# K's cache ahead of the MLP's first weights in the load queue of a one-token decode kernel

## The chip, the cores and the metric

The kernel runs on one core of one Trainium2 chip. The metric is the device time of one execution in microseconds (us). The kernel before took 99.68 us, the median of three runs (99.55, 99.68 and 99.71).

## The reference

One token passes through an attention branch and an MLP branch that both start from the same normalised row; their outputs are added to the row itself.

```python
# x: 1x1x1024; wq: 1024x4096; wo: 4096x1024; w1: 1024x3584; w2: 3584x1024, all bf16
# caches: 1 x 4 heads x 65536 x 128; W = 4096, so only the last 4096 positions count
def _A_ref(x, k_cache, v_cache, wq, wo):
    q = (x @ wq) as 32 heads of 128            # 8 query heads share one cache head
    k, v = the last W rows of each cache head
    p = _softmax(q . k * (Dh ** -0.5))
    return (p @ v, heads side by side) @ wo

def _B_ref(x, w1, b1, w2, b2):
    y = _layernorm(x)
    h = _gelu(y @ w1 + b1)
    return h @ w2 + b2

x = A_x
xn = _layernorm(x)
return x + _A_ref(xn, ...) + _B_ref(xn, ...)
```

The MLP branch normalises a second time: its `y` is the layernorm of `xn`.

## The kernel before

**Work and data.** With one token there is no reuse: each weight and each cache row is read once, 39.86 MB in all. TensorE multiplies the row by the weights in tiles 32 columns wide, four side by side. The order of every engine's instructions is the order in which the program writes them, and all waits are semaphores that are written out by hand.

**The load queue.** All large transfers are issued by SyncE (SP), in this order: W1 (7.34 MB, `w1_p`, line 208), K in two transfers of 2.10 MB (`load_cache(KR, ...)`, line 199), Wq in two of 4.19 MB (`load_rows(WA, wq_p, ...)`, line 191). SP then waits until h is done (line 366) and issues W2 into W1's place (line 367) and V in two transfers of 2.10 MB. It waits until q is done and issues Wo into Wq's place in four transfers of 5.24, 2.10, 0.79 and 0.26 MB. The three small rows, b1 (7 KB), x (2 KB) and b2 (2 KB), are issued by ScalarE, in this order, on a queue of its own (lines 204 to 206).

**The row.** x arrives (semaphore `s_xrow`); TensorE turns it into a column (line 289); VectorE, GpSimd and ScalarE do both layernorms on it (lines 292 to 316), which gives `XNTb` for q and `YTb` for h. VectorE then clears half of PSUM (line 318).

**h.** TensorE adds b1 (line 353) and waits for `YTb` and for W1; a rolled loop does 8 steps of 7 products (`h_rows`, line 358). ScalarE copies the result (373, 374), TensorE turns it (392), VectorE copies it to `HT` (397) and goes through GELU in small steps (401 to 413) with one exponential on ScalarE (406).

**K.** K's two transfers land in `KR`. VectorE turns them in 8 pieces of 128x2048 (`turn_k`, line 326) from `KR` into `KD`, which lies 2048 columns ahead of `KR` in the same buffer, so that each piece is written over the piece before it, which has been read by then. A piece that starts a transfer (n = 0 and n = 4) waits for that transfer; the others wait for the piece before. In VectorE's order pieces 0 to 2 stand behind line 318, piece 3 between the two halves of GELU, and pieces 4 to 7 behind GELU.

**q and the rest.** TensorE waits for `HT` (line 419), lays a mask into PSUM (422) and does q in two parts of four steps, each when its half of Wq has landed: SP passes on the landing (`s_row`, lines 370, 371). Then follow the turn of q (427 to 450), the scores on `KD` (477), the softmax (480 to 513), h by W2 (515), p by V (528), and the product with Wo (564 to 572), whose rows are taken as Wo's four transfers land. ScalarE copies the sum (579) and writes it out (581).

Of the kernel before, what the change touches and what calls it, by code (L numbers as in the profile page):

```python
# [10 lines left out]
D = 1024  # L11
# [39 lines left out]
def bass_parallel_sum__sliding_block_cached__mixer_channel_mlp__decode_kernel(  # L51
# [18 lines left out]
    pe, dve, act, pool, sp = nc.tensor, nc.vector, nc.scalar, nc.gpsimd, nc.sync  # L70

    def sems(name, n):
        return [nc.alloc_semaphore(f"{name}{i}") for i in range(n)]

    s_xrow, s_b1, s_b2, s_w1, s_w2, s_out, s_go, s_row = (
        nc.alloc_semaphore(n) for n in ("s_xrow", "s_b1", "s_b2", "s_w1", "s_w2", "s_out", "s_go", "s_row"))
    s_wq = sems("s_wq", len(WQ_CHUNKS))
    s_k = sems("s_k", NPAIR)
# [4 lines left out]
    DVE = Track(nc, "S_DVE")  # L83
# [3 lines left out]
    def sb(name, shape, d):  # L87
        return nc.alloc_sbuf_tensor(name, shape, d)
# [14 lines left out]
    XBR = sb("XBR", [1, 2 * D], bf16)  # L103
# [27 lines left out]
    KR = KV[:, 2048:2048 + HKV * W]  # L131
# [11 lines left out]
    x_row = A_x.rearrange("b s n -> (b s) n")  # L143
# [44 lines left out]
    def load_rows(dst, src, chunks, width, semaphores):  # L188
        c0 = 0
        for j, n in enumerate(chunks):  # L190
            sp.dma_start(  # L191
                dst[:, c0 * width:(c0 + n) * width].rearrange("p (c n) -> p c n", c=n),
                src[:, c0:c0 + n, :],
            ).then_inc(semaphores[j], 16)
            c0 += n

    def load_cache(dst, cache, semaphores):
        for i in range(NPAIR):
            sp.dma_start(  # L199
                dst[:, 2 * i * W:2 * (i + 1) * W],  # L200
                cache[0, 2 * i:2 * i + 2, SK - W:SK, :].rearrange("g (m b) d -> m g (b d)", m=64),
            ).then_inc(semaphores[i], 16)

    act.dma_start(B1R, b1_row.rearrange("o (c n) -> o c n", c=B1N)).then_inc(s_b1, 16)
    act.dma_start(XBR[:, 0:D], x_row).then_inc(s_xrow, 16)
    act.dma_start(XBR[:, D:2 * D], b2_row).then_inc(s_b2, 16)

    sp.dma_start(W1[:, :], w1_p).then_inc(s_w1, 16)  # L208
    load_cache(KR, A_k_cache, s_k)
    load_rows(WA, wq_p, WQ_CHUNKS, NQ, s_wq)  # L210


# [108 lines left out]
    def turn_k(n):  # L321
        if n % 4 == 0:
            dve.wait_ge(s_k[n // 4], 16)
        else:
            dve.wait_ge(DVE.sem, DVE.cnt)
        C["kd"] = DVE.mark(dve.transpose(  # L326
            out=KD4[:, n], in_=KR[:, n * 2048:(n + 1) * 2048].rearrange("p (b e s) -> p b e s", b=16, e=4)))

# [43 lines left out]
    act.wait_ge(PE.sem, C["h"])  # L372
    C["a_hrow"] = ACT.mark(act.activation(out=Hs[:, 0:512], in_=PS[:, 0:512], func=ACTF.Copy))
    C["a_hrow"] = ACT.mark(act.activation(out=Hs[0:96, 512:1024], in_=PS[0:96, 512:1024], func=ACTF.Copy))
    for n in range(3):
        turn_k(n)

    def q_rows(n):
# [11 lines left out]
    for i in range(8):  # L390
        n = 128 if i < 4 else 96
# [9 lines left out]
    DVE.mark(dve.scalar_tensor_tensor(out=U2[:, :], in0=HT[:, :], scalar=0.044715, in1=HT[:, :], op0=ALU.mult, op1=ALU.mult))  # L401
    dve.wait_ge(DVE.sem, DVE.cnt)
    C["d_T"] = DVE.mark(dve.scalar_tensor_tensor(out=U2[:, :], in0=U2[:, :], scalar=1.0, in1=HT[:, :], op0=ALU.add, op1=ALU.mult))
    turn_k(3)
    act.wait_ge(DVE.sem, C["d_T"])
    C["a_sig"] = ACT.mark(act.activation(out=U2[:, :], in_=U2[:, :], func=ACTF.Exp, scale=-GELU_C))
    dve.wait_ge(ACT.sem, C["a_sig"])
# [4 lines left out]
    dve.wait_ge(POOL.sem, C["consts"])  # L412
    C["d_GT"] = DVE.mark(dve.tensor_tensor(out=GT, in0=HT[:, :], in1=U2[:, :], op=ALU.mult))

    for n in range(4, 8):
        turn_k(n)

    pe.wait_ge(DVE.sem, C["zq"])
    pe.wait_ge(DVE.sem, C["d_HT"])
# [193 lines left out]
```

## Time and profile before

| what | value |
|---|---|
| median of three runs | 99.68 us |
| the profiled execution, its own time | 99.53 us |
| its span in the trace | 98.3 us |
| busy: PE, VectorE, ScalarE, GpSimd | 50%, 32%, 10%, 10% of the span |
| time of the DMA packets on the SP queue | 95.1% of 16 engines' span |
| moved | 39.86 MB, mean 406 GB/s |
| first DMA issue on SP | 0.80 us |
| last product's end, write-out issued | 96.15 us, 96.58 us |

The span runs from the first to the last instruction that the profiler saw, in microseconds from its start; the execution's own time is 1.2 us longer. A DMA is seen twice: as the instruction that issues it (SPq for SP, ACTq for ScalarE), with the time which that takes on the issuing engine, and as its packets on the 16 DMA engines. PE is TensorE's products, DVE is VectorE, ACT is ScalarE, POOL is GpSimd.

### The profile page before, as it was taken

Reading aid. Unit: us, or ns where it says so; the run is one execution under the profiler, and the core shown is the slowest. Engines: PE = TensorE matmul, PEld = TensorE weight load, DVE = VectorE, ACT = ScalarE, POOL = GpSimd, SP = SyncE. Lnnn points to the kernel's source line nnn. Section 1 sums busy time; section 2 is a strip of 40 time slices with the busy share of each in tenths; the row PEclk is TensorE's granted clock in tenths of the full one; section 3 lists DMA queues with packets and bytes.
Section 4 is the critical chain, followed back from the end, with each engine's and each line's share of the span. In section 5 each row is a group of like instructions: output and inputs, shape, how many; then the busy total and the mean of one; then the engine's idle time right before and its main releaser. Section 6 shows DMA issues by size and latency. Waiting matters only on the chain.

```text
span 98.3 us, 1233 instructions
## 1 busy us (share of the span) xinstructions
PE 49.0 (50%) x500; PEld 18.4 (19%) x415; DVE 31.5 (32%) x42; ACT 9.6 (10%) x23; POOL 10.1 (10%) x34
## 2 busy tenths in 40 slices
PE   0000022659520700670077589993675599786671
PEld 0000022213110000100010321221433243524240
DVE  0000003270799999993002300415550001300000
ACT  0500000240400000000002200001920001000001
POOL 2000001499940000000000000000000000000000
PEclk9999999999997555559755555999999958999999
DMA  9898888999999999999988889949999979799960
GB/s 350 350 423 373 374 373 374 447 433 427 433 513 440 427 440 440 427 427 427 587 373 373 373 373 513 607 173 427 427 433 513 467 333 533 317 417 427 387 267 1
DMA packets 1773, 39.86 MB, mean 406 GB/s; under 512 B 231, under 2 KB 235, under 8 KB 493
## 3 DMA queue, kind: packets, MB, share of 16 engines
q1 hardware_dynamic: 1728, 39.85, 95.1%
q10 hardware_dynamic: 44, 0.01, 0.1%
q14 instruction: 1, 0.00, 0.0%
HBM read 39.86 MB, written 0.00 MB: 406 GB/s over the span
## 4 chain that ended last, share of the span: by engine, by line
DMA 89%; PE 4%; SPq 4%; issue 1%; ACT 0%
DMA WW<-in_A_wq_dram 47%; DMA WW<-in_A_wo_dram 42%; PE PS L334 4%; SPq L191 2%; SPq L199 1%; ACT ORow L579 0%; SPq L208 0%; SPq L370 0%
## 5 line engine op out<-in xcount | busy, mean ns | idle before, releaser
L326 DVE STREAM_TRANSPOSE KV<-KV 128x2048 bf16<-128x2048 bf16 x8 | 18.5, 2310 | 3.4 <-DMA KV<-in_A_k_cache_dram 3.2
L334 PE MATMUL PS<-WW,XNTb 128*32 x64 | 7.2, 629 | 11.9 <-SPq L370 11.9
L334 PE MATMUL PS<-WW,VEC 128*32 (+1 forms) x240 | 9.5, 275 | 4.9 <-issue 3.2
L334 PE MATMUL PS<-KV,LB 128*128 128x512 bf16 x31 | 9.0, 463 | 1.1 <-DVE LB L450 1.1
L289 PE MATMUL PS<-oneb,XBR 1*128 1x1 bf16 x8 | 0.6, 196 | 13.9 <-DMA XBR<-in_A_x_dram 13.9
L334 PEld LDWEIGHTS PS<-WW,VEC 128*32 (+1 forms) x236 | 5.1, 96 | 9.3 <-issue 9.0
L334 PE MATMUL PS<-KV 128*64 x32 | 5.3, 507 | 1.9 <-DMA KV<-in_A_v_cache_dram 1.9
L334 PE MATMUL PS<-WW,YTb 128*32 x56 | 5.1, 494 | 1.5 <-DMA WW<-in_B_w_dram 1.5
L480 DVE TENSOR_REDUCE MXP<-PS 128x1 f32<-128x1024 f32 x2 | 2.4, 1224 | 8.3 <-PE PS L334 8.3
L292 DVE COPY XT<-PS 128x8 f32<-128x8 f32 x1 | 0.2, 168 | 14.6 <-PE PS L289 14.6
L334 PEld LDWEIGHTS PS<-WW,XNTb 128*32 x32 | 1.2, 114 | 18.4 <-issue 18.4
L541 DVE SCALAR_TENSOR_TENSOR OD<-PS,BLK,OD 128x128 f32<-128x128 f32 x3 | 1.1, 351 | 10.6 <-ACT OD L538 10.5
L334 PE MATMUL PS<-OUTM,PAR 2*128 2x512 bf16 x4 | 1.9, 614 | 4.7 <-DVE HT L397 4.7
L534 PE MATMUL PS<-E,identf 128*128 128x512 f32 x8 | 3.9, 616 | 0.0
L427 DVE CAST Qs<-PS 128x512 bf16<-128x512 f32 x1 | 0.7, 691 | 8.4 <-PE PS L334 8.4
L334 PEld LDWEIGHTS PS<-KV,LB 128*128 128x128 bf16 x16 | 1.9, 117 | 7.7 <-issue 6.9
L510 DVE STREAM_TRANSPOSE KV<-KV 128x512 bf16<-128x512 bf16 x4 | 2.7, 712 | 1.8 <-ACT KV L506 1.8
L334 PEld LDWEIGHTS PS<-KV 128*64 x32 | 2.4, 142 | 4.5 <-issue 4.0
L289 PEld LDWEIGHTS PS<-oneb,XBR 1*128 1x128 bf16 x8 | 0.6, 165 | 13.9 <-issue 13.9
L506 ACT ACTIVATE KV<-PS,BIAS 128x512 bf16<-128x512 f32 x4 | 2.7, 685 | 0.0
L425 ACT ACTIVATE Qs<-PS 128x512 bf16<-128x512 f32 x1 | 0.6, 597 | 20.4 <-PE PS L334 20.4
L334 PEld LDWEIGHTS PS<-WW,YTb 128*32 x32 | 1.5, 107 | 5.4 <-issue 5.2
(93 smaller groups left out, 37.6 us busy)
## 6 DMA issues: line engine op xcount, KB each, us to landing
WW<-in_B_w_dram SPq DMA_DIRECT2D x2, 7168.0 KB, 29.9
WW<-in_A_wq_dram SPq DMA_DIRECT2D x2, 4096.0 KB, 41.7
WW<-in_A_wo_dram SPq DMA_DIRECT2D x1, 5120.0 KB, 35.0
KV<-in_A_k_cache_dram SPq DMA_DIRECT2D x2, 2048.0 KB, 26.0
KV<-in_A_v_cache_dram SPq DMA_DIRECT2D x2, 2048.0 KB, 47.1
WW<-in_A_wo_dram SPq DMA_DIRECT2D x1, 2048.0 KB, 39.5
WW<-in_A_wo_dram SPq DMA_DIRECT2D x1, 768.0 KB, 40.9
WW<-in_A_wo_dram SPq DMA_DIRECT2D x1, 256.0 KB, 41.1
```

The costliest lines, as they stand in the source:

```text
L191: sp.dma_start(dst[:, c0 * width:(c0 + n) * width].rearrange("p (c n) -> p c n", c=n), src[:, c0:c0 + n, :],).then_inc(semaphores[j], 16)
L199: sp.dma_start(dst[:, 2 * i * W:2 * (i + 1) * W], cache[0, 2 * i:2 * i + 2, SK - W:SK, :].rearrange("g (m b) d -> m g (b d)", m=64),).then ...
L289: last = pe.matmul(xt[:, r:r + 1], lhsT=XBR[0:1, r:D:KC], rhs=oneb[0:1, 0:1])
L326: C["kd"] = DVE.mark(dve.transpose(out=KD4[:, n], in_=KR[:, n * 2048:(n + 1) * 2048].rearrange("p (b e s) -> p b e s", b=16, e=4)))
L334: return pe.add_instruction(mybir.InstMatmult(name=nc.get_next_instruction_name(), engine=pe.engine, ins=[lowered(rhs, False), lowered(lhs ...
L425: C["a_qs"] = ACT.mark(act.activation(out=Qs[:, 0:512], in_=PS[:, 6 * 512:7 * 512], func=ACTF.Copy))
L427: C["d_qs"] = DVE.mark(dve.tensor_copy(Qs[:, 512:1024], PS[:, 7 * 512:8 * 512]))
L480: C["mx", half] = DVE.mark(dve.tensor_reduce(out=MXP[:, half:half + 1], in_=PS[:, half * 1024:(half + 1) * 1024], axis=AX.X, op=ALU.max))
L506: C["exp"] = ACT.mark(act.activation(out=Pb[:, n * 512:(n + 1) * 512], in_=PS[:, n * 512:(n + 1) * 512], func=ACTF.Exp, bias=BIAS[:, :], s ...
L510: C["tr", n] = DVE.mark(dve.transpose(out=PT.rearrange("p (i c h) -> p c i h", i=NPAIR, h=16)[:, 16 * n:16 * n + 16], in_=Pb[:, n * 512:(n ...
L534: pe.matmul(PS[:, 3 * 512:4 * 512], lhsT=identf[:, :], rhs=E4[:, 0:512])
L541: C["d_od"] = DVE.mark(dve.scalar_tensor_tensor(out=OD[:, :], in0=PS[:, 4 * 512 + 128 * c:4 * 512 + 128 * c + 128], scalar=BLK[:, c:c + 1] ...
```

## The change

K's two transfers are issued ahead of W1's on SP; x's load is issued ahead of b1's on ScalarE. On VectorE all 8 pieces of K stand together, ahead of the copy to `HT` and of GELU. Every piece now waits for VectorE's own instruction before it; pieces 0 and 4, which waited for their transfer alone, wait for both. No instruction is added or removed, and no tile, size or operand changes.

```diff
+    act.dma_start(XBR[:, 0:D], x_row).then_inc(s_xrow, 16)
     act.dma_start(B1R, b1_row.rearrange("o (c n) -> o c n", c=B1N)).then_inc(s_b1, 16)
-    act.dma_start(XBR[:, 0:D], x_row).then_inc(s_xrow, 16)
     act.dma_start(XBR[:, D:2 * D], b2_row).then_inc(s_b2, 16)
 
+    load_cache(KR, A_k_cache, s_k)
     sp.dma_start(W1[:, :], w1_p).then_inc(s_w1, 16)
-    load_cache(KR, A_k_cache, s_k)
     load_rows(WA, wq_p, WQ_CHUNKS, NQ, s_wq)
...
     def turn_k(n):
         if n % 4 == 0:
             dve.wait_ge(s_k[n // 4], 16)
-        else:
-            dve.wait_ge(DVE.sem, DVE.cnt)
+        dve.wait_ge(DVE.sem, DVE.cnt)
         C["kd"] = DVE.mark(dve.transpose(
             out=KD4[:, n], in_=KR[:, n * 2048:(n + 1) * 2048].rearrange("p (b e s) -> p b e s", b=16, e=4)))
...
-    for n in range(3):
+    for n in range(8):
         turn_k(n)
...
     C["d_T"] = DVE.mark(dve.scalar_tensor_tensor(out=U2[:, :], ...))
-    turn_k(3)
     act.wait_ge(DVE.sem, C["d_T"])
...
     C["d_GT"] = DVE.mark(dve.tensor_tensor(out=GT, in0=HT[:, :], in1=U2[:, :], op=ALU.mult))
 
-    for n in range(4, 8):
-        turn_k(n)
```

## The prediction

> **What bounds the kernel now.** I read the page's slices and chain first, then the chain in order of time.
>
> ```profile
> DMA  9898888999999999999988889949999979799960
> GB/s 350 350 423 373 374 373 374 447 433 427 433 513 440 427 440 440 427 427 427 587 373 373 373 373 513 607 173 427 427 433 513 467 333 533 317 417 427 387 267 1
> ...
> DMA 89%; PE 4%; SPq 4%; issue 1%; ACT 0%
> ```
>
> ```profile
> 0.80 0.38 SPq L208
> ...
> 1.24 0.62 SPq L199
> ...
> 1.90 0.67 SPq L199
> ...
> 3.24 46.23 DMA WW<-in_A_wq_dram
> ...
> 54.73 41.08 DMA WW<-in_A_wo_dram
> ```
>
> The DMA engines are busy from end to end, and the chain is 89% transfer. Next I asked whether the load queue ever runs dry. Issue start plus time to landing, from the list of DMA issues taken issue by issue, gives the landings: W1 0.80 + 19.4 = 20.2, K 25.1 and 30.0, Wq 39.8 and 49.5, W2 66.4, V 71.3 and 76.2, Wo 88.4, 93.3, 95.2 and 95.8 us. Behind W1 that is 39.85 - 7.34 = 32.51 MB in 75.6 us, 430 GB/s, and each step by itself is at that rate: K 2.10 MB in 4.90 us, Wq 4.19 in 9.71, W2 7.34 in 16.97. The order of issue is the order of landing and nothing waits between. (The 173 GB/s slice is a matter of counting: a packet's bytes are booked where the packet starts.) So the end is set by three things alone: when the stream starts, its bytes, and the 0.35 us from the last landing to the last product with the write-out behind it. Reckoned back from W1's landing by W2's 16.97 us, the stream's effective start is 20.23 - 16.97 = 3.26 us.
>
> How it starts, in slices of 0.2 us, shows the first packets 1.0 us after W1's issue began (0.80) and 0.63 us after it ended (1.18):
>
> ```profile
> 1.60:1.80 0.20, 0.00 (x0) 0.00 (x0) 0.00 (x0) 0.00 (x0) 0.00 (x0) 1.00 0.00 0
> 1.80:2.00 0.20, 0.00 (x0) 0.00 (x0) 0.00 (x0) 0.00 (x0) 0.00 (x0) 1.00 7.31 2294
> ```
>
> Last come the engines' timelines, VectorE's rows and then TensorE's, and one row of the waits:
>
> ```profile
> 25.16 7.00 DVE L326 STREAM_TRANSPOSE KV<-KV 128x2048 bf16<-128x2048 bf16 x3 [3.21 <-DMA KV<-in_A_k_cache_dram]
> ...
> 35.66 9.34 DVE L326 STREAM_TRANSPOSE KV<-KV 128x2048 bf16<-128x2048 bf16 x4
> ```
>
> ```profile
> 20.81 5.12 PE L334 MATMUL PS<-WW,YTb 128*32 x56 [1.52 <-DMA WW<-in_B_w_dram]
> ...
> 32.41 1.86 PE L334 MATMUL PS<-OUTM,PAR 2*128 2x512 bf16 x4 [4.71 <-DVE HT L397]
> 40.06 3.60 PE L334 MATMUL PS<-WW,XNTb 128*32 x32 [5.79 <-SPq L370]
> 49.76 3.60 PE L334 MATMUL PS<-WW,XNTb 128*32 x32 [6.10 <-SPq L370]
> ```
>
> ```profile
> PE PS L334 <- DMA KV<-in_A_v_cache_dram: 1.9, 1, 1.9
> ```
>
> TensorE waits for a landing in every stage; the tightest waits are 1.9 us ahead of V and 0.9 us ahead of Wo.
>
> **The change part by part.**
>
> *The stream's bytes and order.* The same bytes pass, so K lands at about 8.4 and 13.3, W1 at 30.3 (where K's second half landed before), and Wq, W2, V and Wo where they did, all plus the shift of the start. That 16 KB packets stand first and not 57 KB ones costs nothing in rate: K 428 GB/s, W2 432, in either order.
>
> *The start.* This is the one term that reaches the end. The first issue on SP is now K's, not W1's. K's took 0.62 and 0.67 us, W1's 0.38. If packets start 0.63 us after the issue's end, as W1's did (and the write-out's at the end: issue over at 97.18, first packet at 97.82), the stream starts 0.616 - 0.375 = 0.24 us later. Lower bound: V's issue of the same shape took 0.55, and the first issue of a group of alike ones is the cheapest (Wo 0.33 against 0.43 for the next), so K's could be 0.55 - 0.09 = 0.46, a shift of 0.08. Upper bound: 0.67 as K's second, 0.29, and the 16 engines, whose first packets began over 1.81 to 2.57 us, could be spread by the ratio of issues more, 0.77 x (0.62/0.38 - 1) = 0.5, which sums to 0.8. Below nothing: W1's first packets took 2.4 to 3.1 us and not the 2.12 of later ones, so up to 0.25 us (the engine that began last) could be won if small packets fill the pipe sooner. I take 0.24, the row of K itself. K's second issue and W1's end by about 2.6 us, while K's first transfer feeds the engines until 8.4, so these cost nothing; should that cover be gone, 0.4 us for W1's.
>
> *x ahead of b1.* x was landed at 13.8 us. b1's, x's and b2's packets and their semaphore writes each let one W1 packet of 2.12 us pass (data at 6.7, 11.2 and 15.6 us). Between K's packets such a turn is 0.61 us, and x now stands first: I take 5 us, bounds 3 and 13.9. The chain from x to the cleared PSUM took 21.94 - 13.91 = 8.0 us, so it ends at 13, as K's second half lands. All of this lies beside the load of W1, and nothing at the end waits for it.
>
> *All of K on VectorE ahead of HT.* 8 pieces by 2.335 us = 18.7 us, from 13 to 31.7. Queued behind them are `HT`, GELU and q's copies; behind `HT` waits TensorE with the mask and q. h starts 0.58 us behind W1, at 30.9, and takes 5.1 us, or 56/32 x 3.60 = 6.3 if all at half clock: done at 36.0 to 37.2. ScalarE's copies and the turn took 27.70 - 25.93 = 1.8 us: `HT` at 38 to 39, VectorE long free. Mask (1.86 + 0.33) until 40 to 41.2, q's first part (3.60) until 44 to 45, ahead of Wq's second half at 49.7. GELU takes 3.5 us more, to 42, and is needed at 69.
>
> *SP.* Behind h's wait stand W2, V and `s_row`. W2 is issued at 36 to 37.2 and not 26.0, with Wq queued until 49.7: 12 us of cover. V's issues end by 39, ahead of Wq's first landing at 40.0. The two waits on DVE's own semaphore that pieces 0 and 4 gain cost what the others have between them, 2.335 - 2.310 = 0.03 us.
>
> Sum against the profiled execution: 99.53 + 0.24 = 99.77. It lies 0.15 below the median of the runs shown, so for a median 99.68 + 0.24 = 99.92 us.
>
> **The rivals.**
>
> *A, not slower: the start is counted from the issue's beginning.* Both readings fit the one W1 row (1.0 us from its beginning, 0.63 from its end). If descriptors go out as they are made, K's longer issue is hidden behind its own first packets: shift 0, 99.68. It decides if K's first packet stands before 1.9 us. Against it: the write-out's packet came 1.24 us after its issue began and 0.64 after it ended. The Trainium skill, "DMA: Bandwidth & Descriptors", section "Latency and other measured facts", gives one first-byte latency of about 600 ns for such queues and names no shape; with one latency for every shape, counted from the beginning, the sum is 99.68. The trace's 0.63 us agrees with it, but counted from the end.
>
> *B, faster: the pipe fills sooner.* The 0.25 us above is won and the issue's price is not paid: 99.43. It needs both.
>
> *C, VectorE late.* If x landed at X, the pieces end at X + 8.0 + 18.7, and `HT`, mask and first part of q (0.4 + 1.9 + 3.9) at X + 32.9. That reaches 49.7 only at X = 16.8, and V's wait gives another 1.9 us. At X = 13.9 3 us are left. Had x to wait for W1 again (20 us), the price would be about 1.3 us by TensorE, 101.2; Wo, issued at 53.4 for a place at 76.2, would still not be late.
>
> *D, TensorE at half clock at the end.* Granted clock, third figure from the end:
>
> ```profile
> 44.26:47.68 3.41, 0.00 (x0) 0.00 (x0) 0.73 (x1) 0.00 (x0) 0.00 (x0) 1.00 0.98 422
> 47.68:61.33 13.65, 9.33 (x55) 2.53 (x35) 1.48 (x4) 1.13 (x3) 0.00 (x0) 0.50 0.98 425
> 78.40:81.81 3.41, 3.41 (x20) 1.56 (x18) 0.00 (x0) 0.00 (x0) 0.00 (x0) 0.50 1.22 528
> ```
>
> A stretch of idleness is followed by half clock, and work by full. Before, TensorE idles 6.1 us ahead of q's second part; now 49.9 - 44.5 = 5.4. Should that keep it warm, the scores end earlier, the wait for V grows, and V and Wo could meet a cold TensorE. Wo's 16 products take 0.87 us a step with the gap; q's as many columns took 0.90 at half clock, 1.15 with the gap: 8 steps by 0.28 = 2.2, less 0.6 of slack, about 1.6 us, 101.5. Against it: 5.4 us is still longer than a stretch of 3.41. The Trainium skill, "TensorE: Matmul & The Clock Gate", section "Part 1: The HAM clock gate (the "warmup" mystery)", says that one idle window of about 3.4 us, running free of the kernel, gates the clock; by that rule a gap of 5.4 us holds a whole window in 58% of executions, one of 6.1 in 79%. The rows' 3.41 us agrees.
>
> That the change does not do what it says is excluded for order: K's issues stand ahead of W1's on SP and all 8 pieces ahead of `HT` on VectorE.
>
> **How the numbers follow.** 0.2% is 0.20 us, about what a measurement of this kernel can tell from no change. Forecast 0.62: most of its spread (0.08 to 0.8) is above 0.20, so 0.44 slower, 0.18 the same. A 0.16, the same. B 0.12, faster. C 0.03 and D 0.07, slower. Slower 0.44 + 0.10 = 0.54, same 0.34, faster 0.12. The range goes from 99.55, which takes in A and half of B, to 100.30, which takes in most of the spread and leaves C and D out. The forecast's own range is 99.76 to 100.3.
>
> **What would show it.** In the profile after: K's issue first on SP, 0.6 us long; first packets near 2.05 us; K landed at 8.4 and 13.3, W1 at 30.3, Wo's last part 0.24 us later than 95.81; VectorE through with K by 33 us; TensorE's waits for Wq, V and Wo still there. First packets at 1.8 us say A. An empty stretch in the DMA row or a wait of TensorE for VectorE behind 49 us says that I am wrong about the cover, and a last row that ends later than 0.4 us after Wo's last landing says D.

## The result and the profile after

The changed kernel took 99.95 us (median of 8 runs, 99.86 to 100.3) against 99.60 us for the kernel before (8 runs, 99.44 to 99.71): ratio 1.0042, 95% interval 1.0028 to 1.0056. It is slower by 0.35 us, and the interval does not reach 1. The forecast was 99.92 us, slower. The profiled execution took 100.02 us with a span of 98.8 us, against 99.53 and 98.3.

The page's slices for the kernel after:

```profile
DMA  2799999988899999999998889949999899799960
GB/s 54 292 428 438 451 458 627 441 372 372 372 411 425 425 438 451 478 451 425 567 441 372 372 372 418 627 196 425 425 431 557 382 415 531 315 408 431 382 268 1
```

The row is as full as before, but for the first slice: 54 GB/s where 350 stood. Much of that drop is counting. A packet's bytes are booked where it starts, and K's packets have 16 KB where W1's had 57. The chain in order of time shows where the stream begins and ends:

```profile
0.80 0.63 SPq L199
...
2.11 1.08 SPq L209
...
55.28 41.03 DMA WW<-in_A_wo_dram
```

K's issue takes 0.63 us. The last transfer lands at 55.28 + 41.03 = 96.31 us, against 54.73 + 41.08 = 95.81: 0.50 us later, which is the whole difference of the two profiled executions (100.02 - 99.53 = 0.49). The slices of 0.2 us (the last two figures are the DMA share and GB/s) show that this was there from the first packet on:

```profile
2.00:2.20 0.20, 0.00 (x0) 0.00 (x0) 0.00 (x0) 0.00 (x0) 0.00 (x0) 1.00 0.00 0
2.20:2.40 0.20, 0.10 (x2) 0.13 (x3) 0.00 (x0) 0.00 (x0) 0.00 (x0) 1.00 3.44 655
```

K's first packet starts at 2.21 us, where W1's started at 1.81. VectorE and TensorE, in their timelines, and one row of the waits:

```profile
10.46 18.81 DVE L325 STREAM_TRANSPOSE KV<-KV 128x2048 bf16<-128x2048 bf16 x8
39.49 0.26 DVE L396 CAST HT<-PS 128x16 f32<-128x16 bf16 x2 [10.22 <-PE PS L391]
```

```profile
31.16 6.53 PE L333 MATMUL PS<-WW,YTb 128*32 x56 [22.56 <-DMA WW<-in_B_w_dram]
...
41.06 3.28 PE L333 MATMUL PS<-WW,XNTb 128*32 x32
50.31 3.60 PE L333 MATMUL PS<-WW,XNTb 128*32 x32 [5.97 <-SPq L369]
```

```profile
PE PS L333 <- DMA KV<-in_A_v_cache_dram: 3.8, 1, 3.8
```

VectorE has turned all of K at 29.3 us and then stands idle for 10 us until h's sum has been turned. q's second part waits for Wq as before, and TensorE's wait for V is longer, not shorter (3.8 against 1.9 us). No engine became late for the stream.

### The profile page after: what moved, and what is told of

It is laid out like the page before. It is cut to its first block, busy times and chain, and to the rows that moved or that the text cites. A ratio compares the mean times of both kernels' runs of the same rounds, so it can differ in the third digit from the quotient of the medians.

```text
span 98.8 us, 1236 instructions
## 1 busy us (share of the span) xinstructions
PE 48.2 (49%) x501; PEld 18.6 (19%) x415; DVE 31.8 (32%) x42; ACT 9.6 (10%) x23; POOL 10.1 (10%) x34
## 4 chain that ended last, share of the span: by engine, by line
DMA 88%; SPq 4%; PE 4%; issue 1%; ACT 0%
DMA WW<-in_A_wq_dram 47%; DMA WW<-in_A_wo_dram 42%; PE PS L333 4%; SPq L191 2%; SPq L199 1%; SPq L209 1%; ACT ORow L575 0%; SPq L369 0%
## 5 line engine op out<-in xcount | busy, mean ns | idle before, releaser
L333 PE MATMUL PS<-WW,YTb 128*32 x56 | 6.5, 594 | 22.6 <-DMA WW<-in_B_w_dram 22.6
L333 PE MATMUL PS<-WW,VEC 128*32 (+1 forms) x240 | 10.5, 310 | 4.7 <-SPq L558 1.8
L333 PE MATMUL PS<-KV,LB 128*128 128x512 bf16 x32 | 7.1, 379 | 0.7 <-DVE LB L446 0.7
L333 PEld LDWEIGHTS PS<-WW,VEC 128*32 (+1 forms) x236 | 5.6, 104 | 9.6 <-issue 9.0
L372 ACT ACTIVATE Hs<-PS 128x512 bf16<-128x512 f32 x1 | 0.6, 597 | 28.6 <-PE PS L333 28.6
L215 POOL TENSOR_SCALAR_AFFINE_SELECT OUTM<-OUTM 2x512 bf16<-2x512 bf16 x1 | 2.3, 2302 | 0.1
L318 DVE MEMSET PS<- 128x2048 f32 x1 | 1.8, 1765 | 0.4 <-issue 0.4
```

What stands on the lines that cost most here:

```text
L215: return POOL.mark(pool.affine_select(out=out, in_=out, pattern=pattern, compare_op=op, fill=value, base=base, channel_multiplier=step))
L318: C["zq"] = C["zo"] = DVE.mark(dve.memset(PS[:, 4 * 512:8 * 512], 0.0))
L333: return pe.add_instruction(mybir.InstMatmult(name=nc.get_next_instruction_name(), engine=pe.engine, ins=[lowered(rhs, False), lowered(lhs ...
```

## The experiments

In the table, "first packets" has the times at which the first and the 16th packet of the load stream began. The trace does not name a packet's engine: in `k_one_run` and `w1_bytes_as_k` an engine had ended its first packet by then, so the 16 may include second ones. "Last landing" is when the first and the last of the 16 DMA engines were done with Wo's last part. Both come from one profiled execution each; for `k_order_alone`, `w1_piece_leads` and `k_in_plain_quarters` that was the longest of their executions, 0.3 to 0.4 us above the median. Ratios are against the kernel before on the same chip. The experiments ran on four chips, and the whole change was repeated on one of them only, beside `one_run_small_later` and `w1_piece_small_later`.

| run | ratio (95% interval) | first packets, us | last landing, us |
|---|---|---|---|
| the kernel before | 1 | 1.81 to 2.57 | 95.33 to 95.81 |
| the kernel after | 1.0042 (1.0028 to 1.0056) | 2.21 to 3.12 | 95.73 to 96.30 |
| whole_change_again | 1.0026 (1.0015 to 1.0037) | 2.25 to 2.78 | 95.62 to 96.31 |
| k_order_alone | 1.0036 (1.0025 to 1.0048) | 2.21 to 3.19 | 95.93 to 96.41 |
| all_but_k_order | 0.9995 (0.9984 to 1.0007) | 1.80 to 2.83 | 95.30 to 95.89 |
| w1_piece_leads | 0.9999 (0.9987 to 1.0011) | 1.80 to 2.35 | 95.36 to 95.94 |
| w1_piece_small_later | 0.9986 (0.9975 to 0.9997) | 1.81 to 2.35 | 95.31 to 95.85 |
| k_in_plain_quarters | 1.0034 (1.0022 to 1.0045) | 2.15 to 2.34 | 95.88 to 96.20 |
| small_loads_later | 1.0019 (1.0007 to 1.0031) | 2.24 to 3.27 | 95.86 to 96.19 |
| k_one_run | 1.0023 (1.0011 to 1.0035) | 1.82 to 3.03 | 95.37 to 96.21 |
| one_run_small_later | 1.0024 (1.0011 to 1.0037) | 1.82 to 2.58 | 95.30 to 96.33 |
| w1_bytes_as_k | 1.0042 (1.0025 to 1.0059) | 1.82 to 2.67 | 95.31 to 96.34 |
| x_on_sp_first | 1.0070 (1.0042 to 1.0098) | 2.36 to 3.23 | 95.83 to 96.79 |

**Which part of the change costs.** The change was cut in two: K's order alone on the kernel before, and everything else with W1 first.

```diff
# k_order_alone (on the kernel before)
+    load_cache(KR, A_k_cache, s_k)
     sp.dma_start(W1[:, :], w1_p).then_inc(s_w1, 16)
-    load_cache(KR, A_k_cache, s_k)
# all_but_k_order (on the kernel after)
+    sp.dma_start(W1[:, :], w1_p).then_inc(s_w1, 16)
     load_cache(KR, A_k_cache, s_k)
-    sp.dma_start(W1[:, :], w1_p).then_inc(s_w1, 16)
```

> K's two transfers ahead of W1's on SP, and nothing else of the change: b1's load stays ahead of x's, and VectorE's pieces of K stay where they were. Theory S (the start: all of the loss is that the stream starts later because K's issue comes first): the same loss as the whole change, +0.35 us in the median within 0.1, ratio 1.0035, first packet near 2.2 us and last landing near 96.3 us in the trace. Rival V (part of the loss comes from VectorE's order or x's load): less than half of it, ratio under 1.0018.

> x's load ahead of b1's and all 8 pieces of K on VectorE ahead of HT, with W1 first on SP as before. Theory S: no loss, ratio 1.000 within 0.001, first packet at 1.8 us and last landing at 95.8 us, although VectorE turns K from 25 to 44 us, HT stands at 44 and q's first part ends only near 50, since Wo is issued at 54 for a place at 76. Rival V: a loss of 0.2 us or more, ratio 1.002 or more, seen as a later issue of Wo or later waits for V.

K's order alone gave 1.0036, the rest 0.9995. The loss is K's order; VectorE's and x's moves together cost nothing that can be measured (at most 0.07% by the interval). The second run is also the hard case for VectorE's order, since K lands at 25 us there. Its chain:

```profile
1.24 23.97 DMA KV<-in_A_k_cache_dram
...
41.72 2.31 DVE KV L325
...
44.28 5.40 PE PS L333 x36
...
49.84 2.90 PE PS L333 x28
...
54.08 41.81 DMA WW<-in_A_wo_dram
```

VectorE turns K until 44.0 us, `HT` comes behind it at 43.96 and q's first part ends at 49.68, as expected. The chain of waits now runs through K and VectorE, yet Wo is issued at 52.8 and lands at 95.9. V's last landing, behind which Wo's packets stand, comes at 76.3, so about 23 us of cover are left, as the prediction had it for Wo (53.4 and 76.2).

**A transfer of another form in front.** A quarter of W1 is issued ahead of K.

```diff
# w1_piece_leads (on the kernel after)
+    sp.dma_start(W1[:, 0:2 * F], w1_p[:, 0:2 * F]).then_inc(s_w1, 16)
     load_cache(KR, A_k_cache, s_k)
-    sp.dma_start(W1[:, :], w1_p).then_inc(s_w1, 16)
+    sp.dma_start(W1[:, 2 * F:KC * F], w1_p[:, 2 * F:KC * F]).then_inc(s_w1, 16)
...
-    pe.wait_ge(s_w1, 16)
+    pe.wait_ge(s_w1, 32)
```

> The whole change, but a quarter of W1 (two of the eight rows of each partition, one plain run of 14 KB a partition) is issued ahead of K, the rest of W1 behind it. Theory S with the pattern of K's transfer as cause (two-level source, long issue): the start is as before, first packets near 1.8 us, ratio 1.000 within 0.0015, though small packets and not 57 KB ones lead. Rival P (small packets fill the DMA engines worse): the loss stays, ratio 1.003 or more. Rival B of the prediction (small packets fill the pipe sooner): a gain, ratio 0.998 or less.

The loss is gone (0.9999), with K still landed at 12.5 and 17.4 us and VectorE's order as in the change. Its slices:

```profile
1.60:1.80 0.20, 0.00 (x0) 0.00 (x0) 0.00 (x0) 0.00 (x0) 0.00 (x0) 1.00 0.40 82
1.80:2.00 0.20, 0.00 (x0) 0.00 (x0) 0.00 (x0) 0.00 (x0) 0.00 (x0) 1.00 3.11 573
```

Packets of 14 KB start at 1.80 us like W1's of 57 KB (the row from 1.60 holds x's 2 KB and the first of them). So it is neither K ahead of most of W1 nor small packets as such that cost, but K's transfer as the first one.

**Dose.** In the kernel before, x's load is moved to SP, ahead of W1.

```diff
# x_on_sp_first (on the kernel before)
-    act.dma_start(XBR[:, 0:D], x_row).then_inc(s_xrow, 16)
...
+    sp.dma_start(XBR[:, 0:D], x_row).then_inc(s_xrow, 16)
     sp.dma_start(W1[:, :], w1_p).then_inc(s_w1, 16)
```

> The kernel before, but x's load stands on SP ahead of W1 and no longer on ScalarE: an issue of 0.2 to 0.5 us is put in front of the stream, and K stays behind W1. If time ahead of the first large issue passes to the end one for one, the loss is that issue with the step to the next, 0.25 to 0.55 us, ratio 1.0025 to 1.0055, and last landing and first packet move alike. If the DMA engines can win it back later: ratio 1.000.

W1's issue moved from 0.80 to 1.20 us, its first packet from 1.81 to 2.36, and the median by 0.72 us. The direction is as expected, the size beyond the 0.25 to 0.55 us: nothing is won back, and the last of the 16 engines lost more (95.81 to 96.79) than the first (95.33 to 95.83). W1's first packet moved by more than its issue did: it came 0.80 us behind the issue's end, where it had been 0.63.

**What of K's transfer.** K's source has two levels (64 rows in each of two heads). Three runs change its form: four transfers of one head each, to every second partition; two transfers of 128 rows that follow one another in one head; and the same from W1's tensor. The last two load as many bytes, but other data.

```diff
# k_in_plain_quarters (on the kernel after)
-    load_cache(KR, A_k_cache, s_k)
+    for i in range(NPAIR):
+        for g in range(2):
+            sp.dma_start(
+                KR[g:128:2, 2 * i * W:2 * (i + 1) * W],
+                A_k_cache[0, 2 * i + g, SK - W:SK, :].rearrange("(m b) d -> m (b d)", m=64),
+            ).then_inc(s_k[i], 16)
...
-            dve.wait_ge(s_k[n // 4], 16)
+            dve.wait_ge(s_k[n // 4], 32)
# k_one_run (on the kernel after)
-    load_cache(KR, A_k_cache, s_k)
+    for i in range(NPAIR):
+        sp.dma_start(
+            KR[:, 2 * i * W:2 * (i + 1) * W],
+            A_k_cache[0, 2 * i, SK - 2 * W:SK, :].rearrange("(m b) d -> m (b d)", m=128),
+        ).then_inc(s_k[i], 16)
# w1_bytes_as_k (on k_one_run)
-            A_k_cache[0, 2 * i, SK - 2 * W:SK, :].rearrange("(m b) d -> m (b d)", m=128),
+            B_w1.rearrange("a b -> (a b)")[i * 128 * 2 * W:(i + 1) * 128 * 2 * W].rearrange("(m n) -> m n", m=128),
```

> The whole change, but K is loaded in four transfers of one head each, whose source has one level of rows (64 rows of 16 KB, to every second partition) in place of two transfers of two heads. Theory S with the pattern as cause: K's first issue takes 0.35 to 0.45 us in place of 0.63, first packets near 1.9 us, loss mostly gone, ratio 1.000 to 1.0015. If it is not the pattern but that K's 16 KB rows come first: ratio 1.003 or more. Three more issues on SP are covered by what is queued in either case.

> The whole change, but each transfer of K reads 128 rows of 16 KB that follow one another in one head (8192 positions of head 0, then of head 2) in place of 64 rows each of two heads: same bytes, same 16 KB packets, same places in SBUF, other data, so the output is not the reference's. If the two levels of K's source are the cause: issue 0.38 us, first packets at 1.8 us, ratio 1.000 within 0.0015. If K's tensor or its 16 KB rows are: ratio 1.003 or more, issue 0.6.

> As k_one_run, but the two first transfers read the first 4.2 MB of W1's tensor, again as 128 rows of 16 KB that follow one another, into K's place (other data, so the output is not the reference's). If the late last engine of k_one_run comes from the form of the read (each engine's eight rows in one run of 128 KB), the last landing is spread over 0.8 to 1.05 us again, first packets at 1.8, ratio 1.002 to 1.003. If it comes from where K's cache lies: spread 0.5 to 0.6, ratio 1.000 within 0.001.

The first quarter was issued in 0.55 us, not in 0.35 to 0.45, and began at 2.15; the ratio was 1.0034. The guess that two levels of the source alone make the issue dear fell, or the step over partitions costs as much. k_one_run was issued in 0.37 us like W1 and began at 1.82 like W1, as the slices of its trace show:

```profile
1.80:2.00 0.20, 0.00 (x0) 0.00 (x0) 0.00 (x0) 0.00 (x0) 0.00 (x0) 1.00 3.72 737
```

So the late first packet (0.40 us) does come with the form of K's transfer. But the loss stayed: the ratio of 1.0023 lies between the two that were expected (at most 1.0015, or 1.003 and more). The first engine was done at 95.37 as before the change, the last at 96.21; the mean of the 16 landings was 95.83, against 95.56 before and 96.02 after the change. What was won for the first engine was not won for the last. w1_bytes_as_k did the same out of another tensor (95.31 to 96.34; its ratio of 1.0042 is above the 1.002 to 1.003 expected), so it is not where K's cache lies. It goes with reading 16 KB rows that follow one another, eight to an engine, as the first thing in the stream. w1_piece_leads, whose 14 KB rows lie 57 KB apart, did not have it; the runs do not separate the rows' length from their distance. Why such a read leaves some engines late was not settled.

**ScalarE's issues beside SP's.** x, b1 and b2 are issued later, on three kernels.

```diff
# small_loads_later (on the kernel after); one_run_small_later is the same on k_one_run
+    act.wait_ge(s_k[0], 16)
     act.dma_start(XBR[:, 0:D], x_row).then_inc(s_xrow, 16)
# w1_piece_small_later (on w1_piece_leads; W1's piece has a semaphore of its own)
+    act.wait_ge(s_p, 16)
     act.dma_start(XBR[:, 0:D], x_row).then_inc(s_xrow, 16)
```

> The whole change, but ScalarE issues its three small loads (x, b1, b2) only when K's first transfer has landed, so that nothing is issued beside SP at the start. Rival C (ScalarE's issues beside SP's lengthen K's issue and hold back its packets): K's issue 0.55 us, first packets at 2.0 us or before, half of the loss gone or more, ratio 1.002 or less. Theory S (K's own transfer sets it): issue 0.6, first packets 2.1 to 2.2 us, ratio 1.003 or more. x lands near 10 us, so y is ready near 17 and VectorE is through with K at 37: hidden in either case.

> k_one_run (K read as 128 rows that follow one another, other data, so the output is not the reference's) with x, b1 and b2 issued only when K's first transfer has landed. Theory: the later start has two parts, the two levels of K's source (first packets at 2.2 instead of 1.8 us) and ScalarE's issues beside 16 KB packets (the engines' first packets spread wider, the last landing 0.84 us behind the first in k_one_run against 0.5 before and 0.33 with the small loads later). Both taken away: ratio 1.000 within 0.001, landings spread by under 0.5 us. If K's 16 KB packets ahead of W1 cost something by themselves: 1.002 or more.

> w1_piece_leads with x, b1 and b2 issued only when W1's leading quarter has landed (about 7 us). If ScalarE's issues at the start widen the spread of the engines, the last engine gains 0.1 to 0.25 us on w1_piece_leads: ratio 0.9975 to 0.999, faster than both kernels. If they do not: 1.000 within 0.001.

> The changed kernel as it is, beside the two others on one chip. All theories: ratio 1.0035 to 1.0045, first packets at 2.2 us, last landing 0.35 to 0.5 us behind that of the kernel before.

In small_loads_later K's issue still took 0.63 us and the first packet still came at 2.24: ScalarE does not delay the start. The ratio of 1.0019 meets the rival's condition (1.002 or less) and the start meets the theory's, so this run alone does not decide; the interval overlaps that of the whole change. Run again beside the last two, the whole change gave 1.0026, less than the 1.0035 to 1.0045 expected. one_run_small_later fell with its theory: ratio 1.0024, landings spread over 1.03 us, so ScalarE's loads do not make the spread either. w1_piece_small_later came out at 0.9986, just clear of one and inside the range expected, but its last landing of 95.85 is no earlier than the 95.81 before, and its interval overlaps that of w1_piece_leads. That it is faster than w1_piece_leads is not shown, nor where its 0.14% against the kernel before comes from.

**W1 in eighths.**

```diff
# w1_in_eighths (on the kernel before)
-    sp.dma_start(W1[:, :], w1_p).then_inc(s_w1, 16)
+    for j in range(8):
+        sp.dma_start(W1[j:128:8, :], w1_p[j:128:8, :]).then_inc(s_w1, 16)
...
-    pe.wait_ge(s_w1, 16)
+    pe.wait_ge(s_w1, 128)
```

> The kernel before, with W1 loaded in eight transfers of every eighth partition (16 rows of 57 KB each, one for each DMA engine). The 16 engines began their first packets over 1.81 to 2.57 us before, over 2.15 to 2.34 where K came in quarters of 64 rows, and the spread stays to the last landing. If the spread comes from the number of packets that an issue makes for each engine, all engines begin within 0.1 us here. With an issue of 0.4 to 0.55 us: first packets at 1.85 to 2.1, the last engine's landing at 95.3 to 95.6, a gain of 0.2 to 0.5 us, ratio 0.995 to 0.998. If the later issues of W1 can't keep the engines fed (eight of 0.45 us against 2.1 us of data each), or the partition step costs as much as is won: ratio 1.000 or more.

It took 118.83 us, ratio 1.1912 (1.1886 to 1.1938), where a gain or no change was expected. W1's 57 KB packets took 4.4 us each and not 2.12, and W1 landed at 39.6 us and not at 20.2; the rest ran at the old rate. The first 16 packets began over 2.19 to 3.74 us, so one packet an engine did not bring the engines closer together. Half the rate came with 16 rows to a transfer that lie eight partitions apart, in SBUF and in the source alike; the runs do not separate the number of rows, the step in SBUF and the step in the source. Every second partition with 64 rows (k_in_plain_quarters) ran at full rate.

## Why the prediction was right

**What bounds the kernel** held. The landings moved together, from K's to Wo's, and x_on_sp_first shows that time put ahead of the stream is lost at the end.

**The stream's start** was the right term, and in the traces too small: 0.24 us from K's issue, against 0.40 for the first packet and 0.50 for the last landing. The medians are less clear, 0.35 us on the first chip and 0.25 on the one where the whole change was repeated. That 99.92 came so near to 99.95 is in part luck: the shift was forecast 0.11 us too small, and was added to a median of 99.68, where the eight runs gave 99.60. K's issue was sized rightly (0.627 against 0.616 us). What failed is the rule of 0.63 us from the issue's end to the first packet, taken from W1 and the write-out: K's came 0.78 us after its issue's end. It was 0.78 to 0.80 also for the first of K's quarters, the first of W1's eighths and for W1 behind x's load, and 0.63 to 0.65 where W1, its piece or k_one_run's K stood first. And the issue's length is not the whole cause, as the prediction put it: k_one_run has W1's issue and W1's first packet, and the last engine is late all the same.

The upper bound, a wider spread of the engines, does not explain the change itself. The first packets spread over 0.91 us in one trace of it (2.21 to 3.12) and over 0.53 in the other (2.25 to 2.78), against 0.76 before, and the last landing was 96.30 and 96.31. Where they spread least, in the quarters (2.15 to 2.34), the last landing was 96.20. The last part of Wo came 0.40 us later on the first engine and 0.49 on the last, so most of the loss is a shift that all engines share. Only in the runs with 16 KB rows that follow one another is the late last engine most of it.

**Rival A** (start counted from the issue's beginning) fell: no packet of K before 2.2 us, 1.4 us after the issue began. By the one first-byte latency of about 600 ns of the Trainium skill ("DMA: Bandwidth & Descriptors", section "Latency and other measured facts"), counted from the issue's beginning and alike for every shape, nothing should have moved. The traces have 1.0 us for W1 and 1.4 us for K from the beginning, and 0.63 and 0.78 us from the end.

**Rival B** (small packets fill the pipe sooner) fell: w1_piece_leads, with 14 KB packets, was at 0.9999.

**VectorE, x and rival C.** x was ready at 2.3 us, outside the bounds of 3 to 13.9: its packet went out before the first of K. VectorE was through at 29.3 us (31.7 was said), h at 37.7 (37.2 at most was said, h's products took 594 ns in the mean against 494 before), q's first part at 44.3. all_but_k_order reached the point at which rival C begins to count: q's first part ended at 49.68 us, 0.14 us behind the landing of Wq's second half. It lost nothing, as the waits for V and the cover of Wo were still there.

**Rival D** did not begin as described, but its later links came in part. The profile after, in four stretches between changes of the granted clock (third figure from the end):

```profile
47.30:54.12 6.82, 3.60 (x32) 0.61 (x16) 0.17 (x1) 0.17 (x1) 0.00 (x0) 0.50 1.11 480
54.12:67.78 13.66, 9.22 (x60) 2.81 (x44) 4.38 (x8) 2.46 (x8) 0.00 (x0) 1.00 0.92 396
78.02:81.43 3.41, 3.41 (x20) 1.55 (x18) 0.00 (x0) 0.00 (x0) 0.00 (x0) 0.50 0.89 384
81.43:98.50 17.07, 11.52 (x164) 5.60 (x156) 1.38 (x5) 0.75 (x2) 0.00 (x0) 1.00 0.80 338
```

The gap ahead of q's second part was 5.97 us and not 5.4, and it did not keep TensorE warm: q's second part ran at half clock again, in 3.60 us as before. The clock rose at 54.12 us, where before it stayed at half until 61.33, so the scores took 7.07 us against 9.03, and the wait for V grew to 3.8 us. Two stretches of half clock followed, from 67.78 to 71.19 beside W2's products, and from 78.02 to 81.43. The product with V took 5.33 us as before, with a half-clock stretch in it both times. Wo's rows ran at full clock: the last row ended 0.34 us after the last landing. The idle window of about 3.4 us that the Trainium skill gives ("TensorE: Matmul & The Clock Gate", section "Part 1: The HAM clock gate (the "warmup" mystery)") agrees with these stretches, which are 3.41 us or multiples of it.

## What to carry to other kernels

Where one load queue is busy from end to end and every other engine waits for it, a new order inside the queue changed nothing at the end of this kernel (w1_piece_leads 0.9999), however much it moved elsewhere. What counted was the first transfer, so put there one that is issued quickly and whose packets start soon on all 16 engines, if only a short piece of it. Engines that wait in every stage can be reordered up to the point where a wait turns round, and that point can be worked out from the trace. Look at the last of the 16 DMA engines too, not at the first packet alone: the end waits for it, and k_one_run won back the first packet and not the time.

## What the runs showed of the hardware

- The spread over which the 16 DMA engines ended the stream's first transfer (0.3 to 1.0 us where that was W1 or K whole) stayed to the end, within about 0.1 us: in w1_bytes_as_k the first transfer landed over 7.67 to 8.70 us and Wo's last over 95.31 to 96.34.
- The form of a transfer changed its issue time as the first one on SP: 0.37 us for 128 rows in one level, 0.63 for 64 rows in each of two heads, 0.55 for 64 rows to every second partition.
- From the issue's end to the first packet 0.63 to 0.65 us passed in some runs and 0.78 to 0.80 in others, also for the same load of W1 (0.63 as the first issue, 0.80 behind x's).
- A transfer of 16 rows whose partitions lie 8 apart ran at half rate (4.4 us for a 57 KB packet against 2.12).
- 16 KB rows that follow one another, at the head of a stream, left the last engine 0.4 to 0.5 us behind where it ended before the change, out of either tensor.
